# One more chunk turned by VectorE, and v loaded and scaled a chunk earlier, in a retention and feed-forward kernel

## The chip, the core and the metric

The kernel runs on one core of a Trainium2 chip. The metric is the device time of one execution in microseconds (us). A core has five engines with an instruction queue each: TensorE (PE in the profile, its weight loads PEld), VectorE (DVE), ScalarE (ACT), GpSimd (POOL) and SyncE (SP), which here does nothing but start DMA transfers. An engine takes its queue in the order in which the program wrote it, and waits on semaphores for the others.

## What is computed

```python
# q, k, v: (8 batches, 8 heads, 576 positions, 64)
scores = scale * np.matmul(q, k.transpose(0, 1, 3, 2))
ret = scores * Dmat            # gamma_head ** (i - j) for j <= i, else 0
attn = np.matmul(ret, v)
x = attn.transpose(0, 2, 1, 3).reshape(4608, 512)
h = np.maximum(x @ w_in, 0.0)          # w_in 512 x 2048
out = h * h @ w_out                    # w_out 2048 x 512
```

The weights come as 64-bit floats, and the kernel rounds them to 32 bits itself.

## The kernel before

**Chunks.** The 4608 rows are taken in 36 chunks of 128 (`N_CH`). Four chunks make a block of 512 rows, for which the first matrix product of the feed-forward part is made. The attention is made chunk by chunk: a running state `u` (heads x 64 x 64) carries what earlier positions of the same batch give; within halves of 64 rows, scores are formed and masked. The decay is taken out of the mask: row by row, q and v are multiplied by factors from a table `dv` (`scale_q`, L396, and `scale_v`, L495; both on GpSimd in the part that matters here), so that the mask is only ones and zeros.

**The main loop** is `for i in range(N_EARLY + 1, N_CH + 1)`, with `N_EARLY` = 4. I call one pass of it iteration i. It writes out, in this order: `move(C, i)` (what is left of the copies of chunk i), `whole(i - 1)` (the attention of chunk i - 1, with the scores of chunk i in between), `turn(i + 1)` for early chunks, `scale_v`, `loads(i)`, `flip(i + 2)` for later chunks, `ffn(i - 1)` (the feed-forward steps that fill the time), and `scale_q`. There is no planner on the chip: the order of each queue is this written order.

**Two ways to bring q and k into the layout with the head dimension on the partitions.** `turn(i)` transposes on TensorE: 16 transposes (L445) into PSUM, then two ScalarE copies to SBUF (L454). `flip(i)` transposes on VectorE in squares of 32: one instruction for k and one for q (L416), put one each into the next two feed-forward steps through the list `flips`; 16 small ScalarE copies (L431) then carry the squares to their partitions. These wait in the list `moves`, and `move(count)` writes out up to `count` of them at the start of a step. `N_TURN` is the first chunk that is flipped.

**Block 0** is special. While chunks 4 to 7 are attended to, each iteration has three feed-forward steps of block 0. One such step is `move(4)`, `convert(6)`, one entry of `flips`, and `step()`. `convert(6)` rounds one 128x512 piece of `w_in`: on VectorE L227, L231, L238, L241, L244, with one ScalarE operation in the middle (L235, between L227 and L241). `step()` is `first_in`: eight matmuls into one of three PSUM tiles `h_ps` (L677), then on ScalarE the square of the previous result (L685) and the ReLU of this one out of PSUM (L683). So ScalarE's queue in a step is: copies L431, L235, L685, L683.

**In `whole`**, TensorE adds the first half of a chunk into the state (`u_ps`, L568), ScalarE copies the state out (`grown`, L501), and only then may TensorE add the second half into the same PSUM tile (L568 again). At the end ScalarE copies the result (L550) and the state once more (L501). Chunk 8 ends a batch with its first half, so `whole(8)` has no such copy in its first part.

**Loads.** q has three buffers, k five and v four, each reused in turn. `loads(i)` loads q and k of chunk i + 3 and v of chunk i + 2. The same SP queue fetches raw weights (L209, L214) and stores results of the feed-forward part to DRAM (L689 and L648). `n_scaled` keeps how far q has been scaled: in iteration i up to chunk i + 2, from iteration `N_TURN` - 3 on up to i + 3.

Of the kernel before, what the change touches and what calls it, by code (L numbers as in the profile page):

```python
# [41 lines left out]
def kernel(  # L42
# [48 lines left out]
    N_CH = n_tok // C  # L91
# [46 lines left out]
    N_EARLY = TOK // C  # L138

    def load(i, names="qkv"):  # L140
        if i == 0:
            nc.sync.dma_start(dv, decays)
        got = loaded.setdefault(i, [None] * 3)
        for name, pool, src in (("q", ld3, q), ("k", ld5, k), ("v", ld4, v)):
            if name not in names:
                continue
            t = got["qkv".index(name)] = pool.tile([128, H, D], F32, tag=name, name=f"{name}_ld")

            issue = nc.scalar if i == 0 and name != "q" else nc.sync
            b, c0 = divmod(i * C, S)  # L150
            runs = [(b, c0, slice(0, C))] if c0 + C <= S else [(b, c0, slice(0, CH)), (b + 1, 0, slice(CH, C))]
            for e in range(1 if name == "v" else 2):
                for b, c0, to in runs:
                    at = src[b, :, c0:c0 + to.stop - to.start, :].rearrange("h s d -> s h d")
                    if name == "v":
                        issue.dma_start(t[to], at)
                    else:
                        issue.dma_start(t[to, e * HP:(e + 1) * HP, :], at[:, e::2, :])
# [174 lines left out]
    def convert(count):  # L333
        for _ in range(count):
            f = next(w_in_steps, None)
            f and f()
# [55 lines left out]
    def scale_q(i, engine, parts=(slice(0, H),)):  # L392
        at = N_PAT + i % N_PAT
        for heads in parts:
            t = loaded[i][0][:, heads, :]
            engine.tensor_tensor(t, t, dv[:, heads, at:at + 1].to_broadcast(list(t.shape)), op=ALU.mult)  # L396
# [1 line left out]

    N_TURN = 9
    ps_t = [None]
    moves = []

# [7 lines left out]
    def flip(i):  # L412
        t = work2.tile([128, 4, 2, HP, 32], F32, tag="flip", name="flip")

        def one(j):
            nc.vector.transpose(t[:, :, j, :, :], loaded[i][j].rearrange("s (p e) (d a) -> s (e d) p a", e=2, d=2))  # L416

        def two():
            one(0)
            to = new_qk(i)  # L420
            for b in range(C // 32):
                for g in range(4):

                    moves.append((i, done[0] + (1 if steps[0][0] == 0 else 2), to[32 * g:32 * g + 32, :, :, 32 * b:32 * b + 32], t[32 * b:32 * b + 32, g, :, :, :]))

        flips.extend([lambda: one(1), two])

    def move(count, i=N_CH):

        while moves and count and moves[0][0] <= i and (moves[0][1] <= done[0] or count == C):  # L430
            nc.scalar.copy(*moves.pop(0)[2:])  # L431
            count -= 1
# [23 lines left out]
    def turn(i, engines=(0, 1)):  # L456
        turn_in(i)
        turn_out(i, engines)
# [33 lines left out]
    def scale_v(i):  # L492
        vs = st[i]["vs"] = loaded[i][2]
        at = i % N_PAT
        nc.gpsimd.tensor_tensor(vs, vs, dv[:, :, at:at + 1].to_broadcast([C, H, D]), op=ALU.mult)  # L495
# [93 lines left out]
    def whole(i):  # L589

        s = st[i]
        xp[0] = ps_x.tile([128, 2, 256], F32, tag="x", name="x_ps", padded_shape=[128, 2, 512])
        clean.clear()
        out_of, into = own_of(i, 0, 1), grow_of(i, 1)
        m = beside_each(out_of, into, (0, 2))[-1]
        beside_each(out_of, into, (4, 6))
        if into:
            grown(i, 1)
        if i + 1 < N_CH:
            scores(i + 1, True)  # L600
            score(i + 1, 0)
            score(i + 1, 1)
        wait_for(m)
        for h in range(2):
            if pos(i, h) == 0:
                continue
            u = u_sb[(2 * i + h) % 3]
            for hp, e, b in HEADS[0:2] + HEADS[4:6] + HEADS[2:4] + HEADS[6:8]:
                m = nc.tensor.matmul(x_at(hp, e, b, h), lhsT=u[rows(e), hp, :], rhs=s["qT"][rows(e), hp, CH * h:CH * h + CH],  # L609
                                     start=clears(b, e), stop=False, skip_group_check=True)  # L610
        out_of, into = own_of(i, 1, 1), grow_of(i + 1, 0)
        beside_each(out_of, into, (0, 2))
        if i + 1 < N_CH:
            score(i + 1, 2)
            score(i + 1, 3)
            masked(i + 1)
        wait_for(m)
        beside_each(out_of, into, (4, 6))
        x_out(i, lambda: grown(i + 1, 0) if into else None)
# [177 lines left out]
    def step():  # L797
        n, f, *args = steps.pop(0)
        done[0] += 1
        f(*args)  # L800
        for _ in range(2 if len(transfers) > 2 else 1):
            if transfers and ahead[0] > QUIET:
                transfers.pop(0)[1]()
# [9 lines left out]
    def ffn(i):  # L813

        if steps and steps[0][0] == 0:

            for _ in range((N_W1 - N_EARLY) * C // TOK):
                move(4)
                convert(6)
                for f in flips[:1]:  # L820
                    f()
                del flips[:1]
                step()
            return
        count = N_MP * NP * C // TOK
        while steps and count:
            held[0] = count <= 1

            due = sum(m[0] <= i + 2 for m in moves)
            move(max(2, min(4, -(-due // (count - 1)))) if count > 1 else 0)  # L830
            ahead[0] = count
            busy[0] = len(flips) > 0
            for f in flips[:1]:
                f()
            del flips[:1]
            step()
            count -= 1
        held[0] = busy[0] = False
        ahead[0] = N_DF
# [6 lines left out]

    def loads(i):
        if i + 3 < N_CH:
            load(i + 3, "qk")
        if i + 2 < N_CH:  # L850
            load(i + 2, "v")

    halves = (slice(0, HP), slice(HP, H))
    warm(5)
# [52 lines left out]
    convert(3)  # L907
    scores(4)
    turn(5, (0, 0))
    load(7, "qk")  # L910
    scale_q(6, nc.gpsimd)
    convert(3)
    step()
# [1 line left out]
    for i in range(N_EARLY + 1, N_CH + 1):  # L915
        move(C, i)
        whole(i - 1)
        if i == N_EARLY + 1:
            convert(4)
        if i + 1 < N_TURN:  # L920
            turn(i + 1, (0, 0))
        if i + 1 < N_CH:
            scale_v(i + 1)
        loads(i)
        if N_TURN <= i + 2 < N_CH:
            flip(i + 2)
        ffn(i - 1)
        for j in range(n_scaled[0], min(i + (4 if i > N_TURN - 4 else 3), N_CH)):
            n_scaled[0] += 1
            scale_q(j, nc.gpsimd)  # L930
# [296 lines left out]
```

## Time and profile before

| | |
|---|---|
| three runs, median (lowest, highest) | 931.35 us (930.88, 931.88) |
| the profiled execution | 931.4 us, of which its span, first to last instruction, 929.7 us |
| busy, share of the span: PE | 922.7 us, 99% |
| PEld | 830.3 us, 89% |
| DVE | 756.2 us, 81% |
| ACT | 346.4 us, 37% |
| POOL | 84.3 us, 9% |
| granted TensorE clock | 0.999 |

Busy time in the iterations around chunk 8, from the view by windows (us):

| iteration | from : to | PE | DVE | ACT | POOL |
|---|---|---|---|---|---|
| 5 | 40.69 : 53.95 | 13.26 | 11.45 | 8.03 | 2.53 |
| 6 | 53.95 : 67.22 | 13.27 | 12.09 | 7.51 | 3.32 |
| 7 | 67.22 : 80.48 | 13.26 | 9.26 | 9.05 | 2.09 |
| 8 | 80.48 : 93.10 | 12.62 | 11.87 | 10.25 | 5.18 |

Times in the views are us from the start of the span. A line of the timeline gives start and length in us, engine, source line, operation, what it writes and reads, and in brackets how long the engine was idle before it and who ended that. In the kernel's timeline an iteration begins where `whole` begins on PE. ScalarE's 37% is a mean over two very unequal parts: after about 480 us it has little to do, while in the iterations of the table it is busy for 7.5 to 10.3 us of 13.

### The profile page before, as it was taken

The page shows a single profiled execution, that of the slowest core. Times are in us where ns is not written, and L with a number is a line of the kernel's source. Part 1 is how long each engine was busy: PE and PEld are TensorE (multiplying, and loading weights), DVE is VectorE, ACT ScalarE, POOL GpSimd, SP SyncE. Part 2 cuts the span into 40 slices and gives each one's busy share as a digit, 9 for nine tenths or more (in the row PEclk, how much of TensorE's full clock was granted, in tenths as well). Part 3 has the DMA queues.
Part 4 walks back from the last instruction along what each step waited for, and adds up shares of the span by engine and source line. Part 5 has one row for each costly group of instructions (what it writes and reads, how often), then busy time and mean ns, then how long its engine had stood idle before and what let it go on. Part 6 is the DMA issues. An engine that isn't in the chain of part 4 may idle for free.

```text
span 929.7 us, 21073 instructions
## 1 busy us (share of the span) xinstructions
PE 922.7 (99%) x8548; PEld 830.3 (89%) x8548; DVE 756.2 (81%) x1215; ACT 346.4 (37%) x788; POOL 84.3 (9%) x84
## 2 busy tenths in 40 slices
PE   8999999999999999999999999999999999999998
PEld 7654888888888888888888899999999999999997
DVE  5888798888898888979876587878888888877887
ACT  3457767667676676676711110000000000000000
POOL 3322111121111111211000000000000000000000
PEclk9999999999999999999999999999999999999999
DMA  9998657678666785784379996566666575465523
GB/s 223 223 258 231 169 150 200 165 212 267 166 182 182 261 216 146 224 267 140 115 255 345 381 334 194 145 165 197 175 165 195 151 209 156 116 177 138 151 85 68
DMA packets 297152, 181.29 MB, mean 195 GB/s; under 512 B 194112, under 2 KB 270016, under 8 KB 296160
## 3 DMA queue, kind: packets, MB, share of 16 engines
q1 hardware_dynamic: 292064, 178.81, 66.4%
q10 hardware_dynamic: 4928, 1.08, 0.6%
q8 instruction: 67, 1.10, 0.5%
q14 instruction: 29, 0.24, 0.1%
q0 software_dynamic: 64, 0.07, 0.0%
HBM read 109.39 MB, written 70.52 MB: 194 GB/s over the span
## 4 chain that ended last, share of the span: by engine, by line
PE 98%; DVE 1%; issue 0%; POOL 0%; ACT 0%; POOLq 0%; DVEq 0%
PE h_b L717 18%; PE o_b L1063 17%; PE h_a L717 12%; PE h_c L717 12%; PE o_c L1063 12%; PE o_a L1063 12%; PE h_ps L677 6%; PE x_ps L574 3%; PE sc_ps L480 2%; PE x_ps L609 1%; PE u_ps L568 1%; PE idle_ps L845 0%; PE t_ps L445 0%; PE sc_ps L509 0%; PE x_ps L535 0%; DVE room L513 0%
## 5 line engine op out<-in xcount | busy, mean ns | idle before, releaser
L717 PE MATMUL h_b<-room,w 128*128 128x256 f32 x768 | 181.5, 379 | 0.0
L431 ACT COPY qk<-flip 32x256 f32<-32x256 f32 x432 | 173.8, 402 | 6.7
L717 PEld LDWEIGHTS h_b<-room,w 128*128 128x128 f32 x768 | 145.8, 190 | 20.0 <-DVE room L736 0.2
L717 PE MATMUL h_a<-room,w 128*128 128x256 f32 x512 | 123.9, 385 | 0.0
L717 PE MATMUL h_c<-room,w 128*128 128x256 f32 x512 | 121.0, 379 | 0.0
L717 PEld LDWEIGHTS h_c<-room,w 128*128 128x128 f32 x512 | 97.3, 190 | 13.2
L717 PEld LDWEIGHTS h_a<-room,w 128*128 128x128 f32 x512 | 95.0, 190 | 13.7
L1063 PE MATMUL o_b<-room,w 128*128 128x192 f32 x496 | 90.7, 326 | 0.0
L1076 ACT COPY r<-o_a 128x192 f32<-128x192 f32 x28 | 8.9, 319 | 209.4 <-PE o_a L1063 209.4
L1063 PEld LDWEIGHTS o_b<-room,w 128*128 128x128 f32 x496 | 82.3, 190 | 0.0
L724 DVE SCALAR_TENSOR_TENSOR room<-room 128x512 f32<-128x512 f32 x96 | 67.2, 700 | 3.3
L396 POOL TENSOR_TENSOR q_ld<-q_ld,dv 128x512 f32<-128x512 f32 x34 | 37.8, 1113 | 286.2 <-DMA q_ld<-in_q_dram 240.7
L1063 PE MATMUL o_a<-a,w 128*128 128x192 f32 x352 | 62.6, 326 | 0.0
L1063 PE MATMUL o_b<-s,w 128*128 128x192 f32 x336 | 61.5, 326 | 0.0
L1063 PE MATMUL o_c<-s,w 128*128 128x192 f32 x336 | 61.5, 326 | 0.0
L1063 PE MATMUL o_c<-room,w 128*128 128x192 f32 x336 | 61.5, 326 | 0.0
L677 PE MATMUL h_ps<-room,w 128*128 128x512 f32 (+1 forms) x152 | 57.7, 532 | 0.6 <-DVE w L244 0.5
L1063 PEld LDWEIGHTS o_a<-a,w 128*128 128x128 f32 x352 | 58.1, 190 | 0.1
L1063 PE MATMUL o_a<-room,w 128*128 128x192 f32 x320 | 56.9, 326 | 0.0
L1063 PEld LDWEIGHTS o_b<-s,w 128*128 128x128 f32 x336 | 55.8, 190 | 0.0
L1063 PEld LDWEIGHTS o_c<-s,w 128*128 128x128 f32 x336 | 55.8, 190 | 0.0
L1063 PEld LDWEIGHTS o_c<-room,w 128*128 128x128 f32 x336 | 55.8, 190 | 0.0
(117 smaller groups left out, 1412.6 us busy)
## 6 DMA issues: line engine op xcount, KB each, us to landing
g_dram<-room SPq DMA_DIRECT2D x164, 256.0 KB, 3.8
a<-g_dram SPq DMA_DIRECT2D x30, 512.0 KB, 5.8
room<-g_dram SPq DMA_DIRECT2D x28, 512.0 KB, 5.1
w_dram<-w SPq DMA_DIRECT2D x28, 448.0 KB, 4.4
w<-w_dram SPq DMA_DIRECT2D x7, 1792.0 KB, 9.6
q_ld<-in_q_dram SPq DMA_DIRECT2D x64, 128.0 KB, 4.1
w<-in_moe_w_in_dram SPq DMA_DIRECT2D x16, 512.0 KB, 6.0
w<-in_moe_w_out_dram SPq DMA_DIRECT2D x64, 128.0 KB, 3.4
```

The lines of the kernel that those rows point to most:

```text
L396: engine.tensor_tensor(t, t, dv[:, heads, at:at + 1].to_broadcast(list(t.shape)), op=ALU.mult)
L431: nc.scalar.copy(*moves.pop(0)[2:])
L480: nc.tensor.matmul(st[i]["sc"][e][rows(h), hp, :], lhsT=st[i]["kT"][rows(e), hp, t], rhs=st[i]["qT"][rows(e), hp, t], start=True, stop=Tru ...
L568: return [lambda hp=hp, e=e, b=b: nc.tensor.matmul(u[rows(e), hp, :], lhsT=loaded[i][1][rows(h), 2 * hp + e, :], rhs=st[i]["vs"][rows(h), ...
L574: return [lambda hp=hp, e=e, b=b: nc.tensor.matmul(x_at(hp, e, b, h), lhsT=s["vs"][rows(h), head(hp, e), :], rhs=s["ret"][rows(h), e, hp, ...
L609: m = nc.tensor.matmul(x_at(hp, e, b, h), lhsT=u[rows(e), hp, :], rhs=s["qT"][rows(e), hp, CH * h:CH * h + CH], start=clears(b, e), stop=F ...
L677: nc.tensor.matmul(p, lhsT=w[:, c, :], rhs=xT[0][:, c, :].rearrange("p (h t) -> p h t", h=2)[:, lo:hi, at[0]:at[1]], start=(c == 0), stop= ...
L717: nc.tensor.matmul(p[:, mm, :], lhsT=w[:, c, :], rhs=xs[n][right][:, c, :], start=(j in OPENS and mm == 0 and c == 0), stop=(j in CLOSES a ...
L724: nc.vector.scalar_tensor_tensor(t, t, 0.0, t, op0=ALU.max, op1=ALU.mult)
L1063: nc.tensor.matmul(p, lhsT=w_out[j][:, m, WO_SLOT[right], :], rhs=s["lefts"][left][:, m, :], start=(i in OPENS and m == 0), stop=(i in CLO ...
L1076: nc.scalar.copy(r[:, 0, LEFT], p)
```

## The change

Chunk 8 is flipped by VectorE and no longer turned by TensorE (`N_TURN` 9 to 8); a step of block 0 writes out up to five of the small copies in place of four; v of a chunk is loaded together with its q and k, one iteration earlier than before; and v of chunk i + 2 is scaled at the end of iteration i, ahead of the next q, in place of early in iteration i + 1. Since the point from which q is scaled a chunk further hangs on `N_TURN`, q of chunk 8 is now scaled in iteration 5.

```diff
-    N_TURN = 9
+    N_TURN = 8
...
             for _ in range((N_W1 - N_EARLY) * C // TOK):
-                move(4)
+                move(5)
                 convert(6)
...
     def loads(i):
         if i + 3 < N_CH:
-            load(i + 3, "qk")
-        if i + 2 < N_CH:
-            load(i + 2, "v")
+            load(i + 3)
...
     turn(5, (0, 0))
-    load(7, "qk")
+    load(7)
     scale_q(6, nc.gpsimd)
...
         if i + 1 < N_TURN:
             turn(i + 1, (0, 0))
-        if i + 1 < N_CH:
+        if i == N_EARLY + 1:
             scale_v(i + 1)
         loads(i)
         if N_TURN <= i + 2 < N_CH:
             flip(i + 2)
         ffn(i - 1)
+        if i + 2 < N_CH:
+            scale_v(i + 2)
         for j in range(n_scaled[0], min(i + (4 if i > N_TURN - 4 else 3), N_CH)):
             n_scaled[0] += 1
             scale_q(j, nc.gpsimd)
```

## The prediction, on record before the changed kernel was run

> **What bounds the kernel now.** I read the chain that ended last first, by engine (page, part 4):
>
> ```profile
> PE 98%; DVE 1%; issue 0%; POOL 0%; ACT 0%; POOLq 0%; DVEq 0%
> ```
>
> The end is set by TensorE alone: time taken out of PE's queue is won, and any new hole in it is lost, one for one. Then who made PE wait, over the whole span:
>
> ```profile
> PE idle_ps L845 <- DVE w L342: 1.1, 1, 1.1
> PE h_ps L677 <- DVE w L244: 0.5, 1, 0.5
> PE x_ps L535 <- DVE room L513: 0.5, 2, 0.3
> PE sc_ps L509 <- DVE qk L454: 0.2, 1, 0.2
> ```
>
> Total, times, longest, in us. All lie before 27 us; the same view from 27 us on is empty. So there is no stall left for the change to cure, none on v or q above all. What remains is PE's own work. The chain in order of time has chunk 8's turn:
>
> ```profile
> 69.34 0.64 PE t_ps L445 x16
> ```
>
> Next I looked for how near other engines are to making PE wait. ScalarE's timeline in iteration 7 and PE's lines at the reuse of `u_ps`:
>
> ```profile
> 67.25 0.60 ACT L683 ACTIVATE room<-h_ps 128x512 f32<-128x512 f32 x1 [1.71 <-PE h_ps L677]
> 67.91 0.37 ACT L501 COPY u_sb<-u_ps 128x256 f32<-128x256 f32 x1
> 69.31 0.59 ACT L550 COPY room<-x_ps 128x512 f32<-128x512 f32 x1 [1.03 <-PE x_ps L574]
> ...
> 77.08 0.60 ACT L683 ACTIVATE room<-h_ps 128x512 f32<-128x512 f32 x1 [1.65 <-PE h_ps L677]
> 77.58 1.63 ACT L431 COPY qk<-flip 32x256 f32<-32x256 f32 x4
> 79.23 0.72 ACT L235 ACTIVATE w<-w,exp_bias 128x512 uint32<-128x512 uint32 x1
> 79.86 0.61 ACT L685 ACTIVATE room<-room 128x512 f32<-128x512 f32 x1
> 80.51 0.60 ACT L683 ACTIVATE room<-h_ps 128x512 f32<-128x512 f32 x1
> 81.17 0.37 ACT L501 COPY u_sb<-u_ps 128x256 f32<-128x256 f32 x1
> ```
>
> ```profile
> 68.42 0.27 PE L568 MATMUL u_ps<-v_ld,k_ld 64*64 64x64 f32 x2
> ...
> 81.69 0.27 PE L568 MATMUL u_ps<-v_ld,k_ld 64*64 64x64 f32 x2
> ```
>
> The copy L501 ends at 67.91 + 0.37 = 68.28, and PE adds the second half at 68.42; the next ends at 81.54, PE goes on at 81.69. In iteration 5, where fewer matmuls lie between, PE shows a gap at just this place: L501 at 41.38 + 0.37 = 41.75, L568 at 41.90. Each time 0.14 to 0.15 us: the hand-over itself. So L501 has no slack. And in front of it ScalarE goes from 77.08 to 81.54 without an idle bracket: with four copies in the step it is just in time.
>
> **What the Trainium skill says.** TensorE: Matmul & The Clock Gate, section "Architectural detail": ScalarE and VectorE are strict FIFO. The trace agrees: at 79.23 L235 stands behind four copies, though VectorE's L241 idles 1.23 us for it. PSUM — Partial Sum Buffer, section "PSUM bank collisions raise a hardware error": accesses of two engines to one bank have to be kept apart by semaphores; that is the 0.15 us pair of L501 and L568. SBUF — State Buffer, section "Who interferes with whom": a VectorE instruction with two SBUF inputs, or in a two-port mode, excludes GpSimd and is excluded by it; with one input outside those modes it isn't. The trace agrees:
>
> ```profile
> 57.04 1.28 DVE L231 TENSOR_SCALAR w<-w 128x512 uint32<-128x512 uint32 x1
> 87.23 0.70 DVE L416 STREAM_TRANSPOSE flip<-k_ld 128x512 f32<-128x512 f32 x1
> ```
>
> L231 takes 0.42 us alone and 1.28 under GpSimd's q at 56.80; the transpose keeps its 0.70 under the one at 86.97.
>
> **The change, part by part.**
>
> *The turn that goes.* 16 transposes: 0.64 us off PE (iteration 7 needs 2.76 us from `whole` to its first h matmul, 69.98 - 67.22; iteration 8, without a turn, 82.60 - 80.48 = 2.12; the difference is 0.64). Also two L454 copies on ScalarE, 1.09 us together. Gain 0.64 us.
>
> *The flip that comes.* Two L416, 0.63 us each start to start, in steps 1 and 2 of iteration 6, and 16 L431 of 0.42 us (86.89 to 88.56 for four), 6.7 us. `move(5)` puts five into step 3 of iteration 6, five into each of steps 1 and 2 of iteration 7, and the last into step 3, followed there by four of chunk 9. Iterations 7 and 8 so get 15 copies each; before, they had 4 and 12. PE doesn't wait for the copies themselves (the last comes about 78 us, the scores of chunk 8 after 80 us), but for what stands behind them: L501.
>
> I walk ScalarE's queue with these distances: five copies 2.09, L235 0.63 (79.23 to 79.86), L685 0.53 (85.77 to 86.29), L683 0.55 (between 0.50 at 77.08 and 0.60 at 86.29).
>
> Iteration 6: on VectorE q 8's scaling no longer blocks L231 at 57.04 (see v below), so piece 9 ends at 59.4 with L241 still behind ScalarE's L235, flip k runs from 60.0 pushing piece 10 to 62.9, flip q 63.55 to 64.25. On ScalarE the ReLU of step 2 starts at 63.82, copies at 64.37, L235 66.46, L685 67.09, L683 67.62, L501 68.2 in place of 67.91. PE loses 0.3; its `whole(6)` ends at 67.22 + 2.12 + 0.3 = 69.64, and h of the three steps is done at 73.1, 76.6 and 80.1 (3.5 us each).
>
> Iteration 7: L550 69.61, L501 70.09, copies 70.48, L235 72.57, L685 73.20, L683 73.73, copies 74.28, L235 76.37, L685 77.00, L683 77.53, the last copy of chunk 8 at 78.08. Chunk 9's copies need VectorE's flip of q 9, and VectorE is itself held by ScalarE: L241 waits for L235 (76.37 + 0.72), so 77.12, L244 77.85, the flip 78.46 to 79.16. Four copies from 79.20, L235 80.87, L685 81.50, L683 82.03, L501 82.58.
>
> L501 at 82.58 in place of 81.17 means PE is 1.41 us late there; the same by parts: -0.64 + 0.3 + 1.75. `whole(8)` has no L501 in its first half, and iteration 8 converts only one piece in place of three, so two L235 fall away and ScalarE, at about 1.7 us of lag, has caught up to PE by the third step. From then on the distance is kept to the end, as PE never waits again.
>
> *Bounds of it.* With 0.60 for L683 the sum is 1.6, with 0.50 it is 1.1. If q 8's scaling still falls on step 1 of iteration 6 and blocks VectorE there, the flip ends at 64.74 and 0.4 is added: 2.0. Should the chunk 9 copies not have to wait for VectorE, 0.7 comes off: 0.7. Below nothing only if L501 isn't held at all.
>
> *v scaled ahead.* GpSimd's queue becomes v7, q7, q8, v8 in place of q7, v7, q8; later always v before the next q. The number of instructions is the same, 1.06 us each. GpSimd idles 10 us per chunk, so nobody waits for it longer. v7 leaves 55.78 for about 49 us, q8 can follow its own load (landing 5.6 us after 46.6 to 47.6) at about 54 us, ahead of step 1 of iteration 6. Cost 0; covered by VectorE's reserve: L244 of piece 8 ends at 55.3 and its matmuls start about 60.2. Piece 6 has the least, ready at 49.5 for 50.45; if v7 lands on it, 0 to 0.8 us for PE, I take 0.
>
> *v loaded ahead.* One transfer of 256 KB more in front of everything from 44 us on: at the 265 GB/s of iteration 5 about 1.0 us, and one issue of 0.5 to 1.0 us on SP. Behind it stand two raw weight fetches (issued 44.29, landing after 5.6 us, wanted by L227 at 52.33): 2.4 us of reserve. v of chunk i + 3 takes the buffer of chunk i - 1, so SP now waits for the end of `whole(i - 1)`. Mostly SP comes there later anyway (q of iterations 10 and 11 issued at 109.89 and 124.53, `whole` over at 109.47 and 123.84). In iteration 9's loads it doesn't: v at 88.33 must wait for about 96.5. Behind it are two stores at 92.66, whose second waits for an ReLU square near 98 anyway, and weights at 98.65. Cost 0, 0 to 0.5 if a store is missed.
>
> **Sum.** The profiled execution is 931.4 us (span 929.7 and 1.7 around it), 0.05 above the median of the runs. 931.35 + 1.4 = 932.8 us. A measurement of this kernel can tell about 0.2%, 1.9 us, from no change: the limits are 929.5 and 933.2. My forecast lies within them, on the slow side.
>
> **Rivals.**
> - *The turn goes and ScalarE hides the rest* (0.12): 931.35 - 0.64 = 930.7. For it: ScalarE is busy only 9.05 of 13.26 us in iteration 7 before. Against it: the idle time lies in front of L683, and L501 has none.
> - *The pile-up, and GpSimd on VectorE's chain* (0.23): q 10 starts at 79.45, 0.3 us after the chain L241, L244, flip on which chunk 9's copies hang. If its load lands before about 78.5 us (it took 10 us from issue), or another GpSimd instruction falls there, L241 or L244 takes 0.85 us longer, as L231 did, and L501 with it: 1.4 + 0.85 = 2.25, 933.6 us. This one is slower by more than 0.2%.
> - *Later trouble* (0.10): chunk 9's copies too late for `whole(8)` (my walk: 92.7 against 94.5) or stores held by SP: 934 and more.
> - That chunk 8 isn't flipped at all is excluded: the order of the queues has no L445 for it, two more L416, and the copies in fives.
>
> **Numbers.** Forecast 0.55, 932.1 to 933.4; the three others as above. The range 931.6 to 934.0 leaves out the first rival and most of the last. Slower by over 0.2%: 0.23, 0.07 of my own upper end and 0.08 of the last, 0.38. Faster: 0.02. Within: 0.60.
>
> **What would show it.** Right: no L445 near 69 us; L501 of `whole(6)` and `whole(7)` late and PE's second L568 just behind it, with gaps of about 0.3 and 1.75 us; ScalarE without idle time from 70 to 82 us; `whole(8)` starting about 1.4 us later than 93.10, and that lag unchanged at 150 us. Wrong: PE's gap at another place, a wait of PE for DVE, or ScalarE idle in front of L501.

## The result, and the profile after

| | before | after |
|---|---|---|
| median, us (lowest, highest) | 931.49 (930.88, 932.2), 12 runs | 933.64 (932.73, 934.0), 12 runs |
| ratio, 95% interval | | 1.0021 (1.0012 to 1.003) |
| the profiled execution, us: time, span | 931.4, 929.7 | 933.18, 931.5 |

The change makes the kernel 2.15 us slower (1.1 to 2.8 by the interval), where I forecast 1.4. From here on, times "of before" that belong to an experiment are those of runs of the kernel before on the same chip as that experiment.

The page of after, parts 1 and 4: the busy times, and the shares of the chain that ended last.

```profile
PE 921.8 (99%) x8532; PEld 829.2 (89%) x8532; DVE 762.3 (82%) x1217; ACT 351.2 (38%) x802; POOL 86.0 (9%) x84
...
PE 93%; DMA 3%; SPq 1%; DVE 1%; POOL 0%; issue 0%; ACT 0%; POOLq 0%; DVEq 0%
```

PE works 0.9 us less than before and the span is 1.8 us longer, so PE now stands still for about 2.7 us more. The waits view of after's PE, from 27 us on, which was empty before, and PE's two lines with those waits:

```profile
PE u_ps L568 <- POOL q_ld L396: 1.5, 1, 1.5
PE u_ps L568 <- ACT u_sb L501: 0.3, 1, 0.3
```

```profile
55.38 0.27 PE L568 MATMUL u_ps<-v_ld,k_ld 64*64 64x64 f32 x2 [0.28 <-ACT u_sb L501]
83.30 0.27 PE L568 MATMUL u_ps<-v_ld,k_ld 64*64 64x64 f32 x2 [1.47 <-POOL q_ld L396]
```

Both are the second half's addition into the state, in the `whole` of iterations 6 and 8. Brackets count only what the profile sees as idle. What a wait costs is better read from the starts of `whole` on PE, for iterations 5 to 9: 40.62, 53.88, 67.15, 80.41 and 93.03 before; 40.33, 53.59, 67.36, 80.32 and 94.64 after. (Those of before lie 0.07 us ahead of the marks in the table of before; the lengths are the same.) Lengths of the iterations worked out from these starts, us (the start of iteration 5 itself differs from one profiled execution to the next by up to 0.9 us, and is not counted here):

| iteration | before | after | difference |
|---|---|---|---|
| 5 | 13.26 | 13.26 | 0.00 |
| 6 | 13.27 | 13.77 | +0.50 |
| 7, without the turn | 13.26 | 12.96 | -0.30 |
| 8 | 12.62 | 14.32 | +1.70 |
| 9 to the last matmul | 831.77 | 831.97 | +0.20 |

The sum is 2.1 us, as the medians have it. ScalarE's timeline of after, at the end of iteration 7 and the start of 8:

```profile
76.72 0.72 ACT L235 ACTIVATE w<-w,exp_bias 128x512 uint32<-128x512 uint32 x1
77.34 0.61 ACT L685 ACTIVATE room<-room 128x512 f32<-128x512 f32 x1
77.86 0.58 ACT L683 ACTIVATE room<-h_ps 128x512 f32<-128x512 f32 x1
78.46 0.40 ACT L431 COPY qk<-flip 32x256 f32<-32x256 f32 x1
79.54 1.65 ACT L431 COPY qk<-flip 32x256 f32<-32x256 f32 x4 [0.68 <-DVE flip L416]
81.22 0.72 ACT L235 ACTIVATE w<-w,exp_bias 128x512 uint32<-128x512 uint32 x1
81.84 0.61 ACT L685 ACTIVATE room<-room 128x512 f32<-128x512 f32 x1
82.36 0.57 ACT L683 ACTIVATE room<-h_ps 128x512 f32<-128x512 f32 x1
82.84 0.36 ACT L501 COPY u_sb<-u_ps 128x256 f32<-128x256 f32 x1
```

This is the queue of my walk: the last copy of chunk 8, an idle bracket for VectorE's flip of q 9, four copies of chunk 9, L235, L685, L683, and L501 ending at 83.20. PE goes on 0.10 us later. But the waits view names another culprit, GpSimd's scaling of q 10, which ran from 81.27 to 82.33 and so ended 0.97 us before PE went on. One of the two is wrong about the larger wait. Iteration 6 holds a wait that I had not put there at all.

### The profile page after: what moved, and what is told of

It is laid out like the page before. It is cut to its first block, busy times and chain, and to the rows that moved or that the text cites. A ratio compares the mean times of both kernels' runs of the same rounds, so it can differ in the third digit from the quotient of the medians.

```text
span 931.5 us, 21037 instructions
## 1 busy us (share of the span) xinstructions
PE 921.8 (99%) x8532; PEld 829.2 (89%) x8532; DVE 762.3 (82%) x1217; ACT 351.2 (38%) x802; POOL 86.0 (9%) x84
## 4 chain that ended last, share of the span: by engine, by line
PE 93%; DMA 3%; SPq 1%; DVE 1%; POOL 0%; issue 0%; ACT 0%; POOLq 0%; DVEq 0%
PE h_b L717 18%; PE o_b L1063 17%; PE h_a L717 12%; PE h_c L717 12%; PE o_c L1063 12%; PE o_a L1063 12%; PE h_ps L677 3%; PE x_ps L574 3%; DMA q_ld<-in_q_dram 2%; PE sc_ps L480 1%; PE x_ps L609 1%; SPq L158 1%; DMA v_ld<-in_v_dram 1%; PE u_ps L568 1%; PE sc_ps L509 0%
## 5 line engine op out<-in xcount | busy, mean ns | idle before, releaser
L431 ACT COPY qk<-flip 32x256 f32<-32x256 f32 x448 | 180.2, 402 | 8.1 <-DVE flip L416 1.1
L396 POOL TENSOR_TENSOR q_ld<-q_ld,dv 128x512 f32<-128x512 f32 x34 | 39.9, 1174 | 277.5 <-DMA q_ld<-in_q_dram 228.2
```

## The experiments

For the wait in iteration 8, my theory is ScalarE's queue: the 15 copies of iteration 7 and the idle time in front of chunk 9's make L501 late. The rival takes the waits view at its word: q 10's scaling on GpSimd, displaced by the new order of v and q, is what PE waits for. For the wait in iteration 6 the question is which half of the change brings it.

### Each half alone

The v half alone (`N_TURN` stays 9, four copies a step):

```diff
-            load(i + 3, "qk")
-        if i + 2 < N_CH:
-            load(i + 2, "v")
+            load(i + 3)
...
-    load(7, "qk")
+    load(7)
...
-        if i + 1 < N_CH:
+        if i == N_EARLY + 1:
             scale_v(i + 1)
...
+        if i + 2 < N_CH:
+            scale_v(i + 2)
```

> Only v's part of the change: v loaded three chunks ahead and scaled two chunks ahead; chunk 8 still turned by TensorE, four copies a step. Theory 1 (PE waits for the state copy L501 behind ScalarE's queue; in iteration 6 because GpSimd's v7 and q7, now back to back at 50 us, hold VectorE and so ScalarE's L235): PE waits about 0.5 us at u_ps near 55 us and nowhere else, 931.5 + 0.5 = 932.0 us. Theory 2 (the profile's name for the 1.5 us wait, GpSimd's q scaling, is the cause, so v's new place in GpSimd's queue does it): the wait of 1.5 us near 82 us is here too, 933.0 us or more.

Measured: 932.33 us against 931.82, ratio 1.0005 (0.9997 to 1.0013). PE's waits from 27 us on, in this kernel:

```profile
PE u_ps L568 <- ACT u_sb L501: 0.8, 1, 0.8
PE h_b L717 <- DVE room L736: 0.2, 1, 0.2
```

The first lies in iteration 6, which takes 14.28 us (+1.01); iteration 8 has no wait, though v and q are scaled in the new order. So the new order doesn't bring the large wait. The interval holds no change, but in this profile the v half isn't free. (Not all of the 1.01 is v's: see what stays open.)

The flip half alone:

```diff
-    N_TURN = 9
+    N_TURN = 8
...
-                move(4)
+                move(5)
```

> Only the flip's part: chunk 8 flipped by VectorE, five copies a step; v loaded and scaled as in the kernel before. Theory 1 (ScalarE's queue): no wait near 55 us, 0.3 to 0.7 us near 68 us, about 1.7 us near 82 us, the turn's 0.64 us won: 931.5 + 1.4 = 932.9 us, 932.6 to 933.3. Theory 2 (GpSimd's new order makes PE wait): the wait near 82 us is gone, 930.9 us.

Measured: 933.43 us against 931.82, ratio 1.0026 (1.0014 to 1.0039). Iteration 8 takes 14.32 us, exactly as in after, and the waits view again gives 1.5 us to L396, now without any change to v. The halves add up, 1.61 + 0.51 = 2.12 us against 2.15 for the whole, though within wide bounds: the v half alone is anywhere from -0.3 to 1.2 us by its interval, and two of the flip half's nine executions lay 3.0 and 4.4 us above its median.

### The flip with the copies paced

Chunk 8's 16 copies are kept in fours, so that iteration 7 writes out 12 in place of 15. Chunk 9's 16 then all fall into iteration 8, in sixes. Against the kernel before:

```diff
-    N_TURN = 9
+    N_TURN = 8
...
-                move(4)
+                move(6 if i == 7 else 4)
```

(`i` is here the argument of `ffn`, one less than the iteration.)

> The flip's part with another pacing of the copies: four a step in iterations 6 and 7 and six in iteration 8 in place of five everywhere, so that no copy of chunk 9 stands in front of the state copy of iteration 8's whole. Theory 1: 12 copies fit in iteration 7, the wait near 82 us goes to under 0.3 us and the one near 68 us to 0.3 or less; the turn's 0.64 us is kept for the most part: 931.1 us, below the kernel before by 0.04%. A theory in which the flip costs by its amount of work on ScalarE and VectorE, and not by where it stands, keeps 932.5 us or more.

Measured: 931.25 us against 931.82, ratio 0.9993 (0.9985 to 1.0001); the waits view from 27 us on is empty. Iterations 6, 7 and 8 take 13.26, 12.62 and 12.58 us. ScalarE, GpSimd's q 10, and PE's second L568, in this kernel at the same place:

```profile
76.83 1.66 ACT L431 COPY qk<-flip 32x256 f32<-32x256 f32 x4
78.52 0.72 ACT L235 ACTIVATE w<-w,exp_bias 128x512 uint32<-128x512 uint32 x1
79.15 0.61 ACT L685 ACTIVATE room<-room 128x512 f32<-128x512 f32 x1
79.67 0.58 ACT L683 ACTIVATE room<-h_ps 128x512 f32<-128x512 f32 x1
80.30 0.37 ACT L501 COPY u_sb<-u_ps 128x256 f32<-128x256 f32 x1
```

```profile
80.10 1.06 POOL L396 TENSOR_TENSOR q_ld<-q_ld,dv 128x512 f32<-128x512 f32 x1 [10.96 <-PE u_ps L568]
```

```profile
80.77 0.24 PE L568 MATMUL u_ps<-v_ld,k_ld 64*64 64x64 f32 x1
```

`whole` starts at 79.54 here. L501 comes 0.76 us after it, as in the kernel before (81.17 - 80.41), and 2.52 in after (82.84 - 80.32). GpSimd is at q 10 from 80.10 to 81.16, and PE goes on at 80.77, in the middle of it: it doesn't wait for q 10. The rival falls; why the waits view names L396 is not shown. With it falls the "DMA 3%" of after's chain: ahead of 83.30 that chain goes through this name and back over q's and v's loads. In this profile, without the wait, the turn's 0.64 us shows up whole.

The same pacing with all of the change:

```diff
-                move(5)
+                move(6 if i == 7 else 4)
```

> The whole change with the copies paced four, four, six as in the run before. Theory 1: the wait near 55 us (0.5 us, v's part) stays, those near 68 and 82 us go: 931.5 - 0.64 + 0.5 = 931.4 us. Theory 2 (GpSimd's order): the wait near 82 us stays, about 933 us.

Measured: 931.74 us against 931.82, ratio 0.9999 (0.9991 to 1.0007). Iterations 6, 7, 8: 13.57, 12.71, 12.58 us. v costs 0.49 us beside the kernel before this one (931.74 - 931.25), as it did alone; the size is rough, as the runs of the two overlap (930.66 to 931.62, and 931.17 to 932.35). In the profile, 0.31 of it lie in iteration 6 and 0.09 in 7.

### How many copies ScalarE can take

Only more copies, with nothing flipped anew:

```diff
-                move(4)
+                move(6)
```

> The kernel before with nothing changed but six copies a step in block 0 in place of four: two more copies, 0.83 us, stand in front of the state copy L501 of iteration 8, and none of the change's other parts is there. Theory 1 (L501 has no slack): PE waits 0.7 to 0.8 us longer near 82 us, 931.8 + 0.75 = 932.5 us. If ScalarE's idle time of 4 us in iteration 7 can hide the copies: 931.8 us.

Measured: 932.42 us against 932.00, ratio 1.0002 (0.9994 to 1.001). The interval holds no change; the profile doesn't: iteration 8 takes 13.13 us, +0.51, and its L568 waits for L501. ScalarE's timeline of this kernel:

```profile
77.85 2.46 ACT L431 COPY qk<-flip 32x256 f32<-32x256 f32 x6
80.34 0.72 ACT L235 ACTIVATE w<-w,exp_bias 128x512 uint32<-128x512 uint32 x1
80.97 0.61 ACT L685 ACTIVATE room<-room 128x512 f32<-128x512 f32 x1
81.49 0.58 ACT L683 ACTIVATE room<-h_ps 128x512 f32<-128x512 f32 x1
81.97 0.36 ACT L501 COPY u_sb<-u_ps 128x256 f32<-128x256 f32 x1
```

Two copies more are 0.83 us, and L501 is 0.53 later against `whole` (81.97 - 80.68 in place of 0.76). The missing 0.30 is in the spacing: here L685, L683 and L501 start 0.52 and 0.48 apart. Before, they were 0.65 and 0.66 apart (79.86, 80.51, 81.17 in the lines of the prediction), because each of the two had waited a moment for PE: L683 for its h, and L501 for the first half of the state, which it copies. The last matmuls of that half, before:

```profile
80.88 0.23 PE L568 MATMUL u_ps<-v_ld,k_ld 64*64 64x64 f32 x2
```

They end at 81.11, and L501 starts at 81.17. In no profiled kernel does L501 of these iterations start less than 0.76 us after `whole`, and wherever ScalarE is early it starts just there; in the paced flip it does so although L683, 0.52 after L685, had not visibly waited. So L501 had about 0.3 us of slack here, hidden in the spacing and in no idle bracket. I had said none.

15 copies in iteration 7, but all of them chunk 8's, so that none waits for VectorE's flip of q 9 (against the kernel before):

```diff
-    N_TURN = 9
+    N_TURN = 8
...
-                move(4)
+                move({5: 1, 6: 5}.get(i, 6))
```

> The flip's part (v as before) with chunk 8's copies paced one in iteration 6, five a step in iteration 7, chunk 9's six a step in iteration 8: iteration 7 again has 15 copies, but none of chunk 9, so none waits for VectorE's flip. Theory 1 splits the 1.7 us wait near 82 us into three copies too many, 1.25 us, and the wait for the flip, 0.5 to 0.7 us: here about 1.2 us are left, 931.25 (the run with 12 copies) + 1.2 = 932.4 us. If the wait for the flip alone did it, 931.3 us; if the number of copies alone, 932.9 us or more.

Measured: 932.33 us against 932.00, ratio 1.0003 (0.9995 to 1.0011). Iteration 8 takes 13.65 us, 1.07 more than the paced flip. That splits the 1.70 us of after: about 1.05 for three copies too many, about 0.65 for the wait on VectorE, which agrees with the idle bracket of 0.68. In this profile the waits view calls PE's wait "issue", a third name for the same copy L501 (81.75 + 0.36 = 82.11, L568 at 82.21).

### What of v costs time

Only the loads a chunk earlier, the scaling in its old place:

```diff
-            load(i + 3, "qk")
-        if i + 2 < N_CH:
-            load(i + 2, "v")
+            load(i + 3)
...
-    load(7, "qk")
+    load(7)
```

> Of v's part only the loads: v loaded three chunks ahead, scaled where it was written before. GpSimd, which runs ahead of PE, then scales v7 as soon as it has landed, near 50 us and behind q7. Theory 1 (what counts is that one more GpSimd instruction falls into iteration 5 and holds VectorE's pieces, so L235, so L501): most of the 0.5 us of v's part is here, 932.2 us. A theory in which the written place of the scaling costs: 931.8 us.

Measured: 934.21 us against 932.00, ratio 1.0021 (1.0012 to 1.0029), 1.7 us more than the whole v half costs (2.21 - 0.51, each over its own runs of before). The expectation, most of 0.5 us, missed. Iteration 6 takes 14.79 us (+1.52, again not all of it v 7's), iterations 5, 29 and 32 take 0.22, 0.38 and 0.64 longer than before. GpSimd and VectorE of this kernel ahead of the wait in iteration 6:

```profile
49.30 1.53 POOL L396 TENSOR_TENSOR q_ld<-q_ld,dv 128x512 f32<-128x512 f32 x1 [4.40 <-DMA q_ld<-in_q_dram]
51.33 1.06 POOL L495 TENSOR_TENSOR v_ld<-v_ld,dv 128x512 f32<-128x512 f32 x1 [0.50 <-DMA v_ld<-in_v_dram]
```

```profile
49.83 1.28 DVE L227 TENSOR_SCALAR w<-w 128x512 uint32<-128x512 uint32 x1
51.04 0.41 DVE L231 TENSOR_SCALAR w<-w 128x512 uint32<-128x512 uint32 x1
51.49 1.45 DVE L238 SCALAR_TENSOR_TENSOR w<-w,w 128x512 f32<-128x512 uint32 x1
```

L227 takes 0.42 us alone and 1.28 here, L238 0.69 and 1.45: each GpSimd instruction holds one of VectorE's. Before, v 7 came only at 55.78, after the pieces that count here. The next L235 on ScalarE waits for VectorE and starts at 54.83; L685, L683 and L501 stand behind it in ScalarE's queue, and L501 starts at 56.46, 2.3 us after the start of `whole` at 54.15, in place of 0.76. After shows the same chain. ScalarE's last L235 of iteration 5 before, and then after's VectorE, GpSimd and ScalarE:

```profile
52.78 0.72 ACT L235 ACTIVATE w<-w,exp_bias 128x512 uint32<-128x512 uint32 x1 [1.20 <-DVE w L227]
```

```profile
50.58 1.43 DVE L244 SCALAR_TENSOR_TENSOR w<-w,w 128x512 uint32<-128x512 uint32 x1
51.93 1.28 DVE L227 TENSOR_SCALAR w<-w 128x512 uint32<-128x512 uint32 x1
```

```profile
50.19 1.27 POOL L495 TENSOR_TENSOR v_ld<-v_ld,dv 128x512 f32<-128x512 f32 x1 [7.03 <-DMA v_ld<-in_v_dram]
51.42 1.50 POOL L396 TENSOR_TENSOR q_ld<-q_ld,dv 128x512 f32<-128x512 f32 x1
```

```profile
53.24 0.72 ACT L235 ACTIVATE w<-w,exp_bias 128x512 uint32<-128x512 uint32 x1 [2.38 <-DVE w L227]
53.87 0.61 ACT L685 ACTIVATE room<-room 128x512 f32<-128x512 f32 x1
54.39 0.58 ACT L683 ACTIVATE room<-h_ps 128x512 f32<-128x512 f32 x1
54.87 0.36 ACT L501 COPY u_sb<-u_ps 128x256 f32<-128x256 f32 x1
```

q 7, scaled at 47.16 before, now stands behind v 7 in GpSimd's queue and follows it at once, so two of VectorE's instructions in a row are held, L235 comes 12.91 us after the start of iteration 5 in place of 12.16, and the stretch ends in the same L501.

The whole change paced, with v 7 alone scaled in its old place (against after):

```diff
-                move(5)
+                move(6 if i == 7 else 4)
...
-        if i == N_EARLY + 1:
+        if i < N_EARLY + 3:
             scale_v(i + 1)
...
-        if i + 2 < N_CH:
+        if N_EARLY + 1 < i and i + 2 < N_CH:
             scale_v(i + 2)
```

> The whole change with the copies paced four, four, six, and the scaling of v7 alone left where it was before, so behind q7 and q8 in GpSimd's queue and out of iteration 5's critical piece; v8 and all later chunks are scaled two chunks ahead, and all loads are three ahead. Theory 1: the wait near 55 us goes, 931.25 us as with the flip alone. If it is the earlier load of v7 (traffic ahead of the raw weights) that costs the 0.5 us, or the scaling ahead in all later chunks: 931.75 us.

Measured: 932.19 us against 932.00, ratio 1.0002 (0.9994 to 1.001). GpSimd of this kernel:

```profile
48.05 1.40 POOL L396 TENSOR_TENSOR q_ld<-q_ld,dv 128x512 f32<-128x512 f32 x1 [4.11 <-DMA q_ld<-in_q_dram]
54.78 1.25 POOL L396 TENSOR_TENSOR q_ld<-q_ld,dv 128x512 f32<-128x512 f32 x1 [5.34 <-DMA q_ld<-in_q_dram]
56.00 2.70 POOL L495 TENSOR_TENSOR v_ld<-v_ld,dv 128x512 f32<-128x512 f32 x2
```

With v 7 away from 50 us, iteration 6 is back at 13.26 us, although v 7 is still loaded early: so in these profiles it is where v 7 is scaled, and not the load as such, that costs in iteration 6. Yet the time is 0.19 us above its own runs of before, where the paced flip's was 0.57 below, so the expectation missed here too. Its profile loses 0.19 us in iteration 7 and 0.44 in iteration 29. The second place is seen best in the v half alone, which loses 0.49 there; its GpSimd, its VectorE and its PE:

```profile
389.62 1.06 POOL L396 TENSOR_TENSOR q_ld<-q_ld,dv 128x512 f32<-128x512 f32 x1 [8.99 <-DMA q_ld<-in_q_dram]
391.71 1.06 POOL L495 TENSOR_TENSOR v_ld<-v_ld,dv 128x512 f32<-128x512 f32 x1 [1.03 <-DMA v_ld<-in_v_dram]
```

```profile
389.82 1.41 DVE L265 TENSOR_TENSOR w<-w 128x512 f32<-128x512 f32 x1
391.15 0.68 DVE L266 TENSOR_TENSOR w<-w 128x512 f32<-128x512 f32 x1
391.87 1.45 DVE L267 TENSOR_TENSOR w<-w 128x512 f32<-128x512 f32 x1
393.24 0.68 DVE L736 TENSOR_TENSOR room<-h_b,room 128x512 f32<-128x512 f32 x1
```

```profile
393.97 1.99 PE L717 MATMUL h_b<-room,w 128*128 128x256 f32 x8 [0.22 <-DVE room L736]
```

Two of three instructions between L731 and L736 are held, and PE waits for L736. Before, the pair of q and v fell at 387.99 and 390.91, mostly beside instructions that read PSUM. No kernel with v in its old place loses anything in iteration 29 (14.36 us in all of them); kernels with v ahead lose 0.04 to 0.49. Why iteration 21 is up to 0.36 us longer than 14.36 in kernels of both kinds, the one before among them (0.09), stays open.

## Why the prediction was right, and where it was not

**The sign, the mechanism and the place of the large wait: right.** The forecast was a wait of PE at the second L568 in the `whole` of iteration 8, behind L501, by copies that stand ahead of it. The wait cost 1.70 us for 1.75. L501 came at 82.84 for 82.58, but that the clock times lie so near is in part luck: after's iteration 5 began 0.29 us earlier than before's, and its iteration 6 lost 0.50 that the walk doesn't have. From the start of iteration 5 to that of `whole(8)` the kernel lost 1.90 us, for 1.4. The paced flip, in which GpSimd still scales q 10 at the very place, shows the cause. The two pieces of the working, copies and VectorE's flip, are both there: about 1.05 and 0.65. Two of my signs went the other way. ScalarE did stand idle between 70 and 82 us, for the 0.68 us that my own walk has there. And PE has a gap at another place, in iteration 6, which I had named as a sign of being wrong; more on it below, under v scaled ahead.

**The turn: right.** 0.64 us. The paced flip's iteration 7 is 12.62 us, 0.64 less than before.

**The small wait at the start of iteration 7: right in size.** I put 0.3 there. In after, L501 starts at 68.56, 1.20 us after its `whole` in place of 0.76, and the iteration loses 12.96 - 12.62 = 0.34; the paced change loses 0.09.

**"So L501 has no slack": wrong by 0.3 us.** I read the row of lines without an idle bracket as a queue without a wait. An instruction that starts right after the one before it can still have waited: L683 and L501 each waited for PE, 0.65 and 0.66 us after the instruction before, and can follow it 0.52 and 0.48 us after. I had taken 0.55 for L683, near the middle of my two ends, so little of this reached the sum.

**v scaled ahead, "I take 0": the term that was mis-sized.** It measures about 0.5 us: 932.33 - 931.82 alone, 931.74 - 931.25 in the paced pair (neither clear of noise by itself), and 0.50 in iteration 6 of after's profile. v 7 came about when I said, 50.19 us for 49. What failed is what I held it against. I compared the converted pieces with the matmuls that read them, 4.9 us of reserve for piece 8. But L235 of each piece stands in ScalarE's queue ahead of L685, L683 and L501, and these have no such reserve. I had read exactly this, VectorE late, L235 late, L501 late, into my walk of iteration 7, and did not use it in iteration 5. I also moved q 7 behind v 7 in GpSimd's queue without asking where q 7's 1.06 us would then fall. Of the 0.75 us by which the forecast was short, this is the most.

**v loaded ahead, 0 to 0.5: not settled.** Loads ahead without the scaling ahead cost 2.21 us, more than both together; in the profile q's and v's scaling then meet other pieces. With v 7 scaled late, the early load left iteration 6 untouched. There the load has no price of its own: it moves GpSimd's instructions, and the price is where they fall. Whether it has one elsewhere is not shown. The second thing that I named, v's load held for the end of `whole(8)`, came as written: issued at 96.70, with no wait of PE near it.

**The rival with GpSimd on VectorE's chain** gave 933.6 us, nearest to the measured time, but not for its reason. It put q 10 at the flip of q 9; q 10 came at 81.27, and L241, L244 and the flip at 77.47, 78.20 and 78.81 kept their 0.69, 0.69 and 0.70 us. The kind of event was right, the place was iteration 5, and it cost 0.5 and not 0.85. *ScalarE hides the rest* needs the copies paced, and is then what is measured: 0.57 us faster, less than one run can tell. *Later trouble* didn't come: from iteration 9 on, after loses 0.20 us.

**What stays open.** The flip half's own profile also lost 0.57 us in iteration 6, while the paced flip, with the same program up to there, lost nothing; in the former v 6 was scaled at 43.59, against an L238 that took 1.43 us, and q 7 at 49.12, in the latter v 6 at 41.70 and q 7 at 47.32. So a loss there can come without v's part, by when a load lands. The profiles of the v half and of the loads alone have the same late v 6 (43.43 and 43.84) beside a long L238, so their 1.01 and 1.52 us are not v 7's alone; in after v 6 came at 42.10 and held no such piece. The 0.5 us of v is a difference of medians over executions and not a constant. The 0.8 us that separate the last kernel from the paced flip, each against its own runs of before, are seen in the profile as 0.19 and 0.44; the rest is not explained.

## What to carry to other kernels

Before work is added to an in-order queue, find the instruction behind it that the bounding engine waits for, and count its slack from starts, not from idle brackets: here 12 small copies fitted into the iteration and 15 cost 1 us, while the gain aimed at was 0.64. When the step ahead of it waits on another engine, that engine's delays belong into the same count, whatever reserve its results have with their last reader. And a name in a view of waits is a suspect until a kernel moves it: here three names stood for one copy.

## What the runs showed of the hardware

- A GpSimd multiplication of 1.06 us (128x512, fp32) holds one VectorE instruction with SBUF operands, in the lines above for 0.74 to 0.86 us: L227 0.42 to 1.28, L244 0.69 to 1.43, L238 0.69 to 1.45. GpSimd's own grows there to as much as 1.53 us. The Trainium skill, SBUF — State Buffer, section "Who interferes with whom", says that whoever comes first gets the shared ports for the whole instruction and the other is blocked; the delays, most of a GpSimd instruction long, agree with it. Which instruction is hit, and so whether PE loses nothing in iteration 6 (the paced flip) or 1.5 us (the loads alone), depends on when q and v land.
- ScalarE starts the copy L501 0.48 us after L683, whose own line is 0.58 us long, when neither waits for PE (six copies a step, after). A wait of L501 for PE of about 0.18 us (0.66 in place of 0.48) leaves no bracket: before, L683 ends at 81.11 and L501 starts at 81.17.
- From the end of L501 on ScalarE to PE's next matmul it takes 0.05 to 0.15 us wherever PE waited for it: 0.06 in iteration 7 of after (68.92 to 68.98), 0.10 in its iteration 8, 0.14 in iteration 8 with six copies a step.
